# Output products by blocks in three more chunks of a fused Performer and MLP kernel, with w_out's sums streamed in and added on GpSimd

## The chip, the cores and the metric

The kernel runs on one core of a Trainium2 chip. The metric is the device time of one execution in microseconds (us), taken as the median of several runs. The engines are named as in the profile: PE is TensorE (PEld its weight loads), DVE is VectorE, ACT is ScalarE, POOL is GpSimd, SP is SyncE, whose queue issues nearly all DMAs here.

## The reference

Attention with positive random features (batch 8, 8 heads, sequence 576, head dimension 64, 128 features), whose result, laid out as 4608 rows of 512, goes through an MLP:

```python
def phi(x):
    proj = np.einsum('bhsd,md->bhsm', x, omega)
    h = proj - np.sum(x * x, axis=-1, keepdims=True) / 2.0
    h = h - np.max(h, axis=-1, keepdims=True)
    return np.exp(h) / np.sqrt(m)
q_p, k_p = phi(q * scale), phi(k * scale)
kv  = np.einsum('bhsm,bhsd->bhmd', k_p, v)
z   = np.sum(k_p, axis=2)
num = np.einsum('bhsm,bhmd->bhsd', q_p, kv)
den = np.einsum('bhsm,bhm->bhs', q_p, z)[..., None] + 1e-06
x   = (num / den).transpose(0, 2, 1, 3).reshape(4608, 512)
h   = x @ w_in                                  # 512 x 2048
out = (h * np.tanh(np.log1p(np.exp(h)))) @ w_out   # 2048 x 512
```

## The kernel before

**Number format.** Every large matrix is held as two fp16 parts, a high part and a rest, and a product takes three matmuls: high by rest, rest by high, high by high. The high parts are casts, mostly on ACT; the rests are a subtraction (`rest`, lines 83 and 85), on DVE for the MLP's activations `g` and `gb`, on GpSimd for `sk`, `sq`, `xs` and `vb`.

**Chunks.** The 4608 rows are 18 chunks of 256. The main loop (line 1284) runs over c = 2 to 17; "iteration c" below means one pass of it. It interleaves two generators: the input product of chunk c (`ff_in`, 8 steps of 24 matmuls 128x256, PE row `ph` of line 770) and the output product of chunk c-1 (`ff_out`, 8 steps of 12 matmuls 128x512, PE row `po` of line 1097). A string of the letters i and o sets the order, one letter for one step. After a number of letters the loop makes a `step()`, which lets the tasks on an agenda emit what is due: the attention of later chunks (k tasks: `pk`, `ek`, `kp`, `pkv`; q tasks: `pq`, `eq`, `qn`, `qp`, `pn`, then `x`), casts and rests. A scheduler then orders what was emitted for each engine; each engine and each queue runs its own list strictly in order.

**Products by blocks.** From chunk 15 (`SC0`, `SO0`) both products are made by the Strassen-Winograd scheme: the operands are cut into 2 by 2 blocks, and seven products of half the size in each direction replace eight. The left and right operands are then blocks (`a11`, `b11` ...) or sums of blocks (`s1` to `s4` of the left, `t1` to `t4` of the right). `ff_in7` makes the input product so, `ff_out7` the output product: 7 products `q_*` of 24 matmuls 128x256 (line 1044), two o steps each. Its left blocks are the tiles `gb`, made by `g_blocks` (casts, 4 subtractions or additions of line 985 for each pair of h tiles, and 14 rests); its results are put together by additions into two `o` tiles (line 1053), each stored once it is whole. The sums of w_in and of w_out are made earlier, in the loop's iterations 4 to 14 (`sums_make`, 10 additions of 128x512 for each of eight pieces, line 806, on DVE) and written to DRAM. `ask_sum` fetches the sums of w_in through a ring of three places (line 878); `fetch_t` fetches all of w_out's sums into tiles that the attention no longer needs (`tw`, line 1015).

**x of the chunks by blocks.** A chunk that takes its input product by blocks needs x transposed in four pieces: the first tile of 128 rows, the second, and two of differences. `x_sums` (line 638) makes the differences `tt` in place and in a tile of the tag "o", and `x_send` sends each piece: a cast into an `xs` tile (2 buffers), the rest on GpSimd, and a transposing DMA from SP (line 616):

```python
tt = sb.tile([P, 2, H * D // 2], F32, tag="o", name=f"tt{c}", bufs=2)
```

The tag "o" has two buffers in SBUF. In `ff_out` an `o` tile lives from its cast at the end of the chunk to its store. In `ff_out7` both are taken at the chunk's start and live to its end. PSUM has three groups: `ps_h` (2 banks: `ph`), `ps_o` (2: `po`, `q_*`), and `ps_a` (4), which serves all of the attention (`pk`, `pq`, `pkv`, `pt`, `pn`) and the products `p_*` of `ff_in7`.

Of the kernel before, what the change touches and what calls it, by code (L numbers as in the profile page):

```python
# [30 lines left out]
def tile_kernel(  # L31
# [11 lines left out]
    P = 128  # L43
# [707 lines left out]
    def ff_in(c):  # L751

        must(2, "x", c)
        sp = [(b_scales(b) if c else None, lo, hi) for b, lo, hi in spans(c * CH, CH)]
        for gr in range(FT // FG):
            gT[c, gr] = sb.tile([P, 2, FG, CH], F16, tag="g", name=f"g{c}_{gr}", bufs=GB)
            for q in range(FG // FQ):
                if c:
                    h = sb.tile([P, FQ, CH], F32, tag="ht", name=f"h{c}_{gr}_{q}", bufs=HB)
                else:  # L760
                    h = g0(gr)[:, q * FQ:(q + 1) * FQ]
                for j in range(0, FQ, 2):
# [12 lines left out]
                    if c == 0:  # L775

                        later(1, cast, act, h[:, j:j + 2, :], ph)
                        if gr == FT // FG - 1 and q == FG // FQ - 1 and j > 0:
                            later(2, mish0)
                    else:  # L780
                        later(1, mish, sp, h[:, j:j + 2, :], ph)
                        if j > 0:
                            later(2, g_split, c, gr, q, sp, h)
                    yield


# [10 lines left out]
    def sums_make(key, blocks, first, shape):  # L797
# [5 lines left out]
        b11, b12, b21, b22 = blocks  # L803

        def tt(out, in0, in1, op=ALU.subtract):
            dve.tensor_tensor(out=out, in0=in0, in1=in1, op=op)
# [196 lines left out]
    def fetch_t():  # L1003
# [7 lines left out]
        for i, (tag, n) in enumerate(places):  # L1011
            t = sb.tile([P, n, 2, BW // 2], F16, tag=tag, name=f"tw{i}", bufs=bufs[tag])
            for u in range(n):
                op, j = units.pop(0)
                nc.sync.dma_start(out=t[:, u], in_=sums["w", j, op])  # L1015
                tsum[op, j] = t[:, u].rearrange("p a (f m) -> p a f m", f=2)

    def ff_out7(c):
        sp = [(b, lo // 2, hi // 2) for b, lo, hi in spans(c * CH, CH)]
        us = o_scale(sp[0][0])[:, 2:3]  # L1020
        if len(sp) > 1:
            mixed = const.tile([P, 1], F32, name=f"uso{c}")
# [8 lines left out]

        def products(name, right):
            n, i = GAT[name]
            own, tag = ((ps_h, "h"), (ps_o, "o"))[nth[0] % 2]
            nth[0] += 1
            ps = own.tile([P, DM // 2], F32, tag=tag, name=f"q_{name}_{c}")
            for f in range(FG):
                must(1, "gb", c, name, f // FQ)
                for a, y in ((1, 0), (0, 1), (0, 0)):
                    if right in full:  # L1040
                        rhs = wo_block(f // 2, y, *full[right])[:, f % 2]
                    else:
                        rhs = tsum[right, f // 2][:, y, f % 2]
                    nc.tensor.matmul(  # L1044
                        out=ps, lhsT=gT[c, n][:, i, a, f, :], rhs=rhs,
                        start=f == 0 and (a, y) == (1, 0), stop=f == FG - 1 and (a, y) == (0, 0),
                    )
# [236 lines left out]
    for c in range(2, NCH):  # L1284
        fi = (ff_in if c < SC0 else ff_in7)(c)
        fo = (ff_out if c <= SO0 else ff_out7)(c - 1)
        order = "io" * 8 if c < SC0 else ("iioiioioioi" if c == SC0 else ORD[c - SO0 - 1]) * 2
        if c == SO0:
            at(slot[0] + 8, fetch_t)
        for j, what in enumerate(order):  # L1290
            if j % 2 == 0 and given[0] < min(pace(c + j / len(order)), len(items)):
                give()
# [53 lines left out]
```

## Time and profile before

| | |
|---|---|
| median of 3 runs | 941.36 us (940.48 to 941.49) |
| the profiled execution | 939.57 us, span 937.8 us |
| PE busy | 920.5 us, 98% of the span |
| PEld busy | 689.4 us, 74% |
| DVE busy | 707.1 us, 75% |
| ACT busy | 658.9 us, 70% |
| POOL busy | 213.6 us, 23% |
| TensorE clock granted, mean | 0.993 |
| DMA | 108.69 MB, mean 116 GB/s |

The difference of 1.8 us between the profiled execution and its span lies before the first and behind the last instruction. In the timeline of PE, iteration 12 begins at 653.0 us, 13 at 701.9, 14 at 751.4, 15 at 799.8 and 16 at 842.

A row of the profile reads: line, engine, operation, out<-in by the program's names, shape, count, then busy time, the mean of one, and the idle time ahead of it with what ended it. In a timeline the first number is the start, the second the duration of the group. DMA issues end with the median time from issue to landing.

### The profile page before, as it was taken

How to read it: one execution, taken by the hardware profiler on the slowest of the kernel's cores; microseconds unless marked ns; L12 is line 12 of the kernel's file. 1: busy time of each engine (PE TensorE's matmuls, PEld its weight loads, DVE VectorE, ACT ScalarE, POOL GpSimd, SP SyncE). 2: the span in 40 equal slices, each digit the busy share in tenths (PEclk: the TensorE clock that was granted, in tenths of full speed). 3: DMA queues.
4: the chain of work that ended last, by engine and by line, in shares of the span. 5: the costliest groups of instructions: out<-in, count | busy, mean ns of one | idle time of the engine just before them, and what ended most of it. 6: DMA issues, size and time to landing. Idle time of an engine off the chain costs nothing. (4 is left out here: it accounts for less than half of the span.)

```text
span 937.8 us, 21111 instructions
## 1 busy us (share of the span) xinstructions
PE 920.5 (98%) x8795; PEld 689.4 (74%) x8795; DVE 707.1 (75%) x1234; ACT 658.9 (70%) x873; POOL 213.6 (23%) x134
## 2 busy tenths in 40 slices
PE   9799989999999999999999999999999999999998
PEld 6688765677777777777777777777777777679997
DVE  5799898685678688787688857878688756658774
ACT  6568966678777878778677776788786866345442
POOL 0000023242342224321333134231241232200000
PEclk9799999999999999999999999999999999999999
DMA  9766325443442256323543265523533156973521
GB/s 308 264 227 215 108 58 93 99 83 75 95 107 85 80 115 128 90 81 76 107 114 97 69 120 107 126 60 93 112 73 91 35 114 141 210 218 92 162 66 45
DMA packets 153055, 108.69 MB, mean 116 GB/s; under 512 B 112832, under 2 KB 125248, under 8 KB 152960
## 3 DMA queue, kind: packets, MB, share of 16 engines
q1 hardware_dynamic: 152640, 106.75, 44.6%
q8 instruction: 69, 1.13, 0.5%
q10 hardware_dynamic: 320, 0.59, 0.2%
q14 instruction: 26, 0.21, 0.1%
HBM read 63.14 MB, written 17.83 MB: 86 GB/s over the span
## 5 line engine op out<-in xcount | busy, mean ns | idle before, releaser
L770 PE MATMUL ph<-xT,w 128*128 128x256 f16 (+1 forms) x2816 | 342.2, 278 | 0.0
L1097 PE MATMUL po<-wo,g 128*128 128x512 f16 x1344 | 308.5, 379 | 0.0
L770 PEld LDWEIGHTS <-w 128*128 128x128 f16 x2688 | 260.7, 98 | 46.1 <-issue 0.6
L1097 PEld LDWEIGHTS <-g 128*128 128x128 f16 x1344 | 127.2, 98 | 132.7
L83 POOL TENSOR_TENSOR sq<-fq,sq 64x1024 f16<-64x1024 f32 x31 | 70.5, 2275 | 253.6 <-ACT sq L74 177.8
L955 ACT ACTIVATE h<-ph,us 128x512 f32<-128x512 f32 (+3 forms) x152 | 83.2, 573 | 49.7 <-PE ph L770 48.5
L85 DVE SCALAR_TENSOR_TENSOR g<-h,us,g 128x1024 f16<-128x1024 f32 (+3 forms) x76 | 99.9, 1325 | 15.2 <-ACT g L74 14.9
L83 POOL TENSOR_TENSOR sk<-fk,sk 64x1152 f16<-64x1152 f32 x24 | 59.3, 2469 | 91.6 <-ACT sk L74 79.3
L83 POOL TENSOR_TENSOR xs<-x,xs 128x512 f16<-128x512 f32 (+1 forms) x35 | 40.7, 1164 | 153.0 <-DVE xs L76 102.0
L955 ACT ACT_TABLE_LOAD x56 | 71.8, 1283 | 1.0
L441 ACT ACT_TABLE_LOAD x53 | 68.0, 1283 | 4.2 <-DVE ek L435 3.3
L426 DVE TENSOR_REDUCE mxq<-pq 128x4 f32<-128x512 f32 x72 | 46.7, 682 | 24.8 <-PE pq L401 23.9
L83 DVE TENSOR_TENSOR qn<-eq,qn 128x1024 f16<-128x1024 f32 x31 | 39.2, 1263 | 29.9 <-ACT qn L74 29.9
L906 PEld LDWEIGHTS <-w 128*128 128x128 f16 x1008 | 59.0, 98 | 3.3 <-issue 0.7
L441 ACT ACTIVATE ek<-ek,lnt 128x1152 f32<-128x1152 f32 x24 | 30.1, 1256 | 42.3 <-DVE ek L435 42.2
L74 ACT ACTIVATE g<-h,us 128x1024 f16<-128x1024 f32 (+3 forms) x64 | 58.2, 932 | 0.8
L426 DVE TENSOR_REDUCE mxk<-pk 128x4 f32<-128x512 f32 (+1 forms) x96 | 49.5, 546 | 7.3 <-PE pk L416 3.5
L83 DVE TENSOR_TENSOR kp<-ek,kp 128x1152 f16<-128x1152 f32 x24 | 32.8, 1366 | 27.0 <-ACT kp L74 26.2
L1044 PEld LDWEIGHTS <-gb 128*128 128x128 f16 x504 | 48.3, 98 | 5.2
L83 POOL TENSOR_TENSOR vb<-vf,vb 128x640 f16<-128x640 f32 x24 | 37.3, 1554 | 55.2 <-DVE vb L76 41.5
L955 ACT ACTIVATE h<-h,us 128x1024 f32<-128x1024 f32 (+2 forms) x16 | 14.7, 930 | 48.6 <-DVE h L915 48.6
L441 ACT ACTIVATE eq<-eq,lnt 128x1024 f32<-128x1024 f32 x31 | 35.6, 1149 | 18.8 <-DVE eq L435 18.5
(185 smaller groups left out, 1370.3 us busy)
## 6 DMA issues: line engine op xcount, KB each, us to landing
w<-ds SPq DMA_DIRECT2D x48, 256.0 KB, 3.6
vf<-in_vL_dram SPq DMA_DIRECT2D x32, 325.0 KB, 3.3
out_dram<-o SPq DMA_DIRECT2D x36, 256.0 KB, 2.3
fq<-in_qT_dram SPq DMA_DIRECT2D x31, 256.0 KB, 3.5
fk<-in_kT_dram SPq DMA_DIRECT2D x24, 256.0 KB, 3.6
raw<-in_w_out_dram SPq DMA_DIRECT2D x5, 1024.0 KB, 7.8
wo<-in_w_in_dram SPq DMA_DIRECT2D x4, 1024.0 KB, 10.6
raw<-in_w_in_dram SPq DMA_DIRECT2D x4, 1024.0 KB, 15.3
```

The costliest lines, as they stand in the source:

```text
L74: act.activation(out, in_, AF.Copy, scale=scale)
L83: eng.tensor_tensor(out=out, in0=in_, in1=hi, op=ALU.subtract)
L85: eng.scalar_tensor_tensor(out=out, in0=in_, scalar=scale, in1=hi, op0=ALU.mult, op1=ALU.subtract)
L426: sub = dve.tensor_reduce(out=mx[:, lo:hi], in_=pp[:, :m, :], axis=AX.X, op=ALU.max, negate=by_act)
L441: last = act.activation(e, e, AF.Exp, bias=lnt)
L770: nc.tensor.matmul(out=ph[:, i, :], lhsT=wi(a, k, f) if c else wi0(k, f), rhs=xT[c][:, y, k, :] if c else xT0()[:, k, :], start=n == 0, st ...
L906: nc.tensor.matmul(out=ph[:, i, :], lhsT=left(gr, op_l, i, a, k), rhs=x_region(c, r)[:, y, k0 + k, :], start=n == 0, stop=n == len(mm) - 1,)
L955: act.activation(h[:, :, lo:hi], ph[:, :, lo:hi], AF.Mish, scale=us[:, 0:1])
L1044: nc.tensor.matmul(out=ps, lhsT=gT[c, n][:, i, a, f, :], rhs=rhs, start=f == 0 and (a, y) == (1, 0), stop=f == FG - 1 and (a, y) == (0, 0),)
L1097: nc.tensor.matmul(out=po[i], lhsT=gT[c, gr][:, a, f % FG, i * P:(i + 1) * P], rhs=wo(y, f), start=f == 0 and (a, y) == parts[0], stop=f = ...
```

## The change

- `SO0` goes from 15 to 12: chunks 12, 13 and 14 take their output product by blocks too. Their input product stays as it was, so `ff_in` now starts `g_blocks` for them in place of `g_split`. In iterations 13 and 14 (output of chunks 12 and 13) the order has 8 i and 14 o; iteration 15 (output of 14) has 14 i and 14 o, where it had 14 i and 8 o.
- The sums of w_out for these chunks are not all held: each is streamed (`ask_t`, two DMAs of 128 KB for each of the four j) into the place of the block `b12` of w_out, which no product reads, as soon as the previous sum has been used there.
- The seven products of chunks 12 and 13 use the two `ps_o` banks only (chunk 14's and later ones alternate between `ps_h` and `ps_o`).
- The additions of `sums_make`, for w_in and w_out alike, go from DVE to GpSimd (line 811 after).
- `fetch_t` is called in iteration 15 as before; its loads land for chunk 15's output product. A scale tile is reused (`spare`).

```diff
-    SO0 = 15
+    SO0 = 12
@@ ff_in
+        hs = {}
         for gr in range(FT // FG):
-            gT[c, gr] = sb.tile([P, 2, FG, CH], F16, tag="g", name=f"g{c}_{gr}", bufs=GB)
+            if c < SO0:
+                gT[c, gr] = sb.tile([P, 2, FG, CH], F16, tag="g", name=f"g{c}_{gr}", bufs=GB)
...
-                        if j > 0:
+                        if j > 0 and c < SO0:
                             later(2, g_split, c, gr, q, sp, h)
+                        elif j > 0:
+                            start(g_blocks(c, gr, q, hs), 2)
@@ sums_make
         def tt(out, in0, in1, op=ALU.subtract):
-            dve.tensor_tensor(out=out, in0=in0, in1=in1, op=op)
+            pool.tensor_tensor(out=out, in0=in0, in1=in1, op=op)
@@
+    T_OPS = ("t3", "t2", "t1", "t4")
+    t_uses = [(c, op) for c in range(SO0, SC0) for op in T_OPS]
+    def ask_t(j):
+        n = t_asked.get(j, 0)
+        t_asked[j] = n + 1
+        if n < len(t_uses):
+            for a in range(2):
+                nc.sync.dma_start(
+                    out=wo_block(j, a, 0, 1),
+                    in_=sums["w", j, t_uses[n][1]][:, a].rearrange("p (f m) -> p f m", f=2),
+                )
@@ ff_out7, products
-            own, tag = ((ps_h, "h"), (ps_o, "o"))[nth[0] % 2]
+            own, tag = ((ps_h, "h"), (ps_o, "o"))[nth[0] % 2 if c + 1 >= SC0 else 1]
...
+                    elif c < SC0:
+                        rhs = wo_block(f // 2, y, 0, 1)[:, f % 2]
...
+                if f % 2 == 1 and right not in full and c < SC0:
+                    ask_t(f // 2)
@@ main loop
-        order = "io" * 8 if c < SC0 else ("iioiioioioi" if c == SC0 else ORD[c - SO0 - 1]) * 2
+        order = "io" * 8 if c <= SO0 else "ioioiooioiooioiooioioo" if c < SC0 else (
+            "iioiioioioi" if c == SO0 == SC0 else ORD[max(0, c - SC0 - 1)]
+        ) * 2
+        if c == SC0:
+            at(slot[0] + 8, fetch_t)
         if c == SO0:
-            at(slot[0] + 8, fetch_t)
+            must(FT // 4, "tsums")
+            for j in range(4):
+                at(slot[0] + 9 + j, ask_t, j)
```

**Where the rows stand now.** Three places show how the lists moved. The first is DVE's list in iteration 14, around the differences `tt15` of chunk 15's x (names carry the chunk or tile and a running number). Before:

```order
L588 TENSOR_TENSOR x31_9748<-pn31_0_9750,rd31_9749 128x256
L588 TENSOR_TENSOR x31_9748<-pn31_1_9775,rd31_9749 128x256
L638 TENSOR_TENSOR tt15_9827<-x31_9748,x30_8879 128x256
L638 TENSOR_TENSOR tt15_9827<-x31_9748,tt15_9827 128x256
L638 TENSOR_TENSOR x31_9748<-x31_9748 128x256
L638 TENSOR_TENSOR x30_8879<-x30_8879,tt15_9827 128x256
L76 CAST xs15_1_9832<-x31_9748 128x512
L76 CAST xs15_2_9863<-tt15_9827 128x512
```

Now:

```order
L1080 SCALAR_TENSOR_TENSOR o13_0_9845<-q_s4_13_10461,warm_74,o13_0_9845 128x256
L990 TENSOR_TENSOR h14_0_1_9924<-h14_1_1_10295,h14_0_1_9924 128x512
L85 SCALAR_TENSOR_TENSOR gb14_2_10370<-h14_0_0_9815,us6_8966,gb14_2_10370 128x512
L85 SCALAR_TENSOR_TENSOR gb14_2_10370<-h14_1_0_10109,us6_8966,gb14_2_10370 128x512
L990 TENSOR_TENSOR h14_0_1_9924<-h14_0_1_9924 128x512
L83 TENSOR_TENSOR qn34_10458<-eq34_10340,qn34_10458 128x1024
L638 TENSOR_TENSOR tt15_10048<-x31_9968,x30_8903 128x256
L85 SCALAR_TENSOR_TENSOR gb14_3_10376<-h14_1_0_10109,us6_8966,gb14_3_10376 128x512
L638 TENSOR_TENSOR tt15_10048<-x31_9968,tt15_10048 128x256
L638 TENSOR_TENSOR x31_9968<-x31_9968 128x256
L638 TENSOR_TENSOR x30_8903<-x30_8903,tt15_10048 128x256
L76 CAST xs15_1_10053<-x31_9968 128x512
```

`tt15` stood right behind the two rows that make x31. It now stands behind the last addition into the first output tile of chunk 13 (`o13_0`), and its first row waits for the store of that tile, whose buffer of the tag "o" it takes; the end of `gb14`, of chunk 14's activations, is now around it.

The second is SP's queue from there on, at the change from iteration 14 to 15. Before (`tw` are loads of `fetch_t`, `xT` and `xm` the pieces of x, `qp` the transposed features of a q tile, the rows of line 878 the ring):

```order
L616 DMA_TRANSPOSE xT15_8409<-xs15_1_9832 128x8x128
L616 DMA_TRANSPOSE xm15_2_9900<-xs15_2_9863 128x8x128
L878 DMA w3_105<-ds2_0_1_7504 128x2x512
L616 DMA_TRANSPOSE xm15_3_9939<-xs15_3_9902 128x4x128
L1015 DMA tw5_10667<-dt1_w_2_5096 128x1024
L1015 DMA tw5_10667<-dt1_w_3_5846 128x1024
L616 DMA_TRANSPOSE xT16_9482<-xs16_0_9995 128x8x128
L558 DMA_TRANSPOSE qp33_10026<-qn33_9970 128x16x128
L1129 DMA out_dram<-o13_0_10127 128x512
```

Now:

```order
L1097 DMA out_dram<-o13_0_9845 128x512
L1035 DMA wo_101<-dt3_w_0_3842 128x2x256 x2
L1035 DMA wo_101<-dt3_w_1_4685 128x2x256 x2
L1035 DMA wo_101<-dt3_w_2_5472 128x2x256 x2
L558 DMA_TRANSPOSE qp34_10508<-qn34_10458 128x16x128
L1035 DMA wo_101<-dt3_w_3_6231 128x2x256 x2
L616 DMA_TRANSPOSE xT15_8408<-xs15_1_10053 128x8x128
L616 DMA_TRANSPOSE xm15_2_10135<-xs15_2_10104 128x8x128
L1035 DMA wo_101<-dt2_w_0_3592 128x2x256
L616 DMA_TRANSPOSE xm15_3_10178<-xs15_3_10137 128x4x128
```

The transposes of x15 stood ahead of the store of `o13_0`; they now stand behind it, behind `qp34`, and among the streamed sums of line 1035. Then follow, in this order, both pieces `xT16` and `xm16_2`, the store of `o13_1`, `xm16_3`, four ring loads, `xT17_0`, `qp35`, and after it `t1`, eight loads of `tw` and `t4`.

The third is DVE's list in iteration 13, from the scores of the k product `pk7_1` to the rest `kp7_1` that its product `pkv7_1` on PE waits for. Before:

```order
L435 TENSOR_TENSOR ek7_1_9062<-pk7_1_4_9073,mxk7_1_9063 128x128
L426 TENSOR_REDUCE mxk7_1_9063<-pk7_1_5_9076 128x4
L85 SCALAR_TENSOR_TENSOR g13_0_8947<-h13_0_0_8948,us5_7600,g13_0_8947 128x4x128
L435 TENSOR_TENSOR ek7_1_9062<-pk7_1_5_9076,mxk7_1_9063 128x512
L85 SCALAR_TENSOR_TENSOR g13_0_8947<-h13_0_0_8948,us6_8942,g13_0_8947 128x4x128
L83 TENSOR_TENSOR kp7_1_9140<-ek7_1_9062,kp7_1_9140 128x1152
```

Now:

```order
L435 TENSOR_TENSOR ek7_1_9139<-pk7_1_4_9150,mxk7_1_9140 128x128
L426 TENSOR_REDUCE mxk7_1_9140<-pk7_1_5_9153 128x4
L435 TENSOR_TENSOR ek7_1_9139<-pk7_1_5_9153,mxk7_1_9140 128x512
L1080 SCALAR_TENSOR_TENSOR o12_0_8997<-q_a12_12_9170,us5_7600,o12_1_8998 128x256
L85 SCALAR_TENSOR_TENSOR gb13_0_9194<-h13_0_0_8971,us5_7600,gb13_0_9194 128x4x64
L85 SCALAR_TENSOR_TENSOR gb13_0_9194<-h13_0_0_8971,us6_8966,gb13_0_9194 128x4x64
L83 TENSOR_TENSOR kp7_1_9215<-ek7_1_9139,kp7_1_9215 128x1152
```

The two rests of `g13` are now rests of `gb13` of half the size, behind the last row of `ek7_1` rather than around it, and an addition of chunk 12's output stands ahead of them. Between `pk7_1` and `pkv7_1`, PE had 3 groups of 12 `po`, 2 of 24 `ph` and the 18 of `pk7_2`; it now has 48 matmuls `q_*` of 128x256, 2 groups of 24 `ph` and the 18 of `pk7_2`.

More of the change, by code (lines that the diff above doesn't have):

```diff
@@ L759, in ff_in @@
                     h = sb.tile([P, FQ, CH], F32, tag="ht", name=f"h{c}_{gr}_{q}", bufs=HB)
+                    hs[gr, q] = h
                 else:
@@ L1016, in fetch_t @@
                 tsum[op, j] = t[:, u].rearrange("p a (f m) -> p a f m", f=2)
+    spare = [warm]
+    T_OPS = ("t3", "t2", "t1", "t4")
+    t_uses = [(c, op) for c in range(SO0, SC0) for op in T_OPS]
+    t_asked = {}
+    def ask_t(j):
[7 more added lines that the diff above has]
+                )
     def ff_out7(c):
@@ L1021, in ff_out7 @@
         if len(sp) > 1:
-            mixed = const.tile([P, 1], F32, name=f"uso{c}")
+            mixed = spare.pop() if spare else const.tile([P, 1], F32, name=f"uso{c}")
             for b, lo, hi in sp:
@@ L1041, in products @@
                         rhs = wo_block(f // 2, y, *full[right])[:, f % 2]
+                    elif c < SC0:
+                        assert t_uses.index((c, right)) == t_asked[f // 2] - 1
+                        rhs = wo_block(f // 2, y, 0, 1)[:, f % 2]
                     else:
```

## The prediction

> **What bounds the kernel now.** I read the page's busy time and digits first, then PE's waits, then a table by iteration.
>
> ```profile
> PE 920.5 (98%) x8795; PEld 689.4 (74%) x8795; DVE 707.1 (75%) x1234; ACT 658.9 (70%) x873; POOL 213.6 (23%) x134
> PE   9799989999999999999999999999999999999998
> ```
>
> PE is busy 98% of the span and full from the eighth slice on. PE's waits between 640 and 842 us, where iterations 12 to 15 lie, are two:
>
> ```profile
> PE p_s L906 <- DVE h L915: 0.6, 1, 0.6
> PE pn L572 <- DMA qp<-qn: 0.5, 1, 0.5
> ```
>
> So PE sets the time, a matmul taken away is worth its time, and no other edit here can gain more than these 1.1 us. A new wait costs its full length. The table by stretch (PE, PEld, DVE, ACT, POOL, clock, DMA share, GB/s) shows iterations 13, 14 and 15:
>
> ```profile
> 702.00:751.00 49.00, 49.00 (x468) 35.36 (x466) 37.29 (x51) 36.51 (x52) 11.67 (x7) 1.00 0.21 60
> 751.00:800.00 49.00, 48.48 (x469) 34.50 (x466) 29.89 (x55) 32.49 (x34) 13.60 (x9) 1.00 0.60 130
> 800.00:842.00 42.00, 41.43 (x489) 29.97 (x487) 25.03 (x54) 16.31 (x28) 5.11 (x5) 1.00 0.91 224
> ```
>
> No other engine is full, but in iteration 15 the DMA engines are 0.91 busy.
>
> **The matmuls: -7.1 us.** Starts in PE's timeline give what each group takes (start, duration, group):
>
> ```profile
> 796.32 1.06 PE L401 MATMUL pq<-om,sq 128*128 128x128 f16 x16
> 797.21 2.75 PE L1097 MATMUL po<-wo,g 128*128 128x512 f16 x12
> 799.80 2.84 PE L906 MATMUL p_a<-xT,w 128*128 128x128 f16 x48
> 802.48 0.91 PE L572 MATMUL pn<-kv,qp 128*128 128x65 f16 x24
> 803.23 2.75 PE L1097 MATMUL po<-wo,g 128*128 128x512 f16 x12
> ...
> 842.84 1.47 PE L1044 MATMUL q_a<-wo,gb 128*128 128x256 f16 x12
> 844.15 1.50 PE L906 MATMUL p_a<-xT,w 128*128 128x128 f16 x24
> ```
>
> Twelve `po` take 799.80 - 797.21 = 2.59 us, twelve `q_` 844.15 - 842.84 = 1.31. A chunk's output goes from 8 x 2.59 = 20.7 to 14 x 1.31 = 18.3, and three chunks from 62.2 to 55.0: -7.1 with the rounding. The other groups move but keep their size: `pq` 0.89, 24 `p_` 1.34 (half of 2.68), `pn` 0.75.
>
> **The new work on DVE and ACT.** Chunk 12, 13 and 14 each get 14 rests (28 of half the width where a chunk spans two batches, as 13 does), 8 additions of h blocks and 8 of output, in place of 4 or 8 rests of `g`:
>
> ```profile
> L85 DVE SCALAR_TENSOR_TENSOR gb<-h,us,gb 128x512 f16<-128x512 f32 x28 | 20.4, 745 | 0.9 <-ACT gb L74 0.2
> L985 DVE TENSOR_TENSOR h<-h 128x512 f32<-128x512 f32 x12 | 8.3, 689 | 4.1 <-ACT h L955 3.9
> L1053 DVE SCALAR_TENSOR_TENSOR o<-q_s,us,o 128x256 f32<-128x256 f32 x12 | 5.6, 480 | 5.8 <-PE q_s L1044 5.7
> L85 DVE SCALAR_TENSOR_TENSOR g<-h,us,g 128x1024 f16<-128x1024 f32 x36 | 58.6, 1627 | 9.9 <-ACT g L74 9.9
> L83 DVE TENSOR_TENSOR qn<-eq,qn 128x1024 f16<-128x1024 f32 x31 | 39.2, 1263 | 29.9 <-ACT qn L74 29.9
> ```
>
> That is 14 x 0.745 + 8 x 0.69 + 8 x 0.48 - 4 x 1.63 = +13 us a chunk, in iterations where DVE has 12 to 19 us free: no bound by its sum, but its queue gets longer where PE waits for it. The tight place is the k product `pkv7_1` in iteration 13:
>
> ```profile
> 710.68 1.17 PE L401 MATMUL pk<-om,sk 128*128 128x128 f16 x18
> 711.68 2.75 PE L1097 MATMUL po<-wo,g 128*128 128x512 f16 x12
> 725.75 1.13 PE L522 MATMUL pkv<-vb,kp 128*128 128x65 f16 x30
> ...
> 724.34 1.36 DVE L83 TENSOR_TENSOR kp<-ek,kp 128x1152 f16<-128x1152 f32 x1 [3.50 <-ACT kp L74]
> ```
>
> PE had 14.0 us of other work from `pk` (done 711.68) to `pkv` (725.75), and DVE's `kp` ended at 725.70: no slack. Now PE has 48 x 0.109 + 2 x 2.62 + 1.0 = 11.5 us there. If the way over DVE and ACT stays 14.0 long, PE waits 2.5 us. The way held one block of 2.1 us that need not return (next part), which leaves none to 0.4. `pkv7_3` stands likewise. Bounds 0 and 5; I take **+1.3**, nearer to the way without the block.
>
> **The sums' additions on GpSimd.** One row of the 80 that leave DVE, what a like operation takes on POOL, and the three rows in which DVE and POOL meet:
>
> ```profile
> L806 DVE TENSOR_TENSOR s<-s,w 128x512 f32<-128x512 f32 x12 | 8.3, 688 | 0.3
> L83 POOL TENSOR_TENSOR xs<-x,xs 128x512 f16<-128x512 f32 x32 | 38.4, 1200 | 140.2 <-DVE xs L76 89.2 <-issue 38.8 <-ACT xs L74 11.6
> ...
> 716.66 2.36 POOL L83 TENSOR_TENSOR sk<-fk,sk 64x1152 f16<-64x1152 f32 x1 [2.58 <-ACT sk L74]
> 716.75 2.83 DVE L85 SCALAR_TENSOR_TENSOR g<-h,us,g 128x512 f16<-128x512 f32 x1
> 720.10 0.74 DVE L85 SCALAR_TENSOR_TENSOR g<-h,us,g 128x512 f16<-128x512 f32 x1
> ```
>
> DVE loses 80 x 0.69 = 55 us or more, POOL gets 80 x 1.2 = 96, spread over ten iterations. DVE's time was not on PE's path, so this gains at most the 1.1 us above. But a `g` rest that starts just behind POOL's `sk` takes 2.83 us, where the next takes 0.74: POOL holds DVE up for the length of its operation. Each of 80 new additions can hold DVE up by 1.2 us, and `sk`, from which `pk` comes, now queues behind up to three of them. Covered by DVE's free time except at the k products without slack; bounds -1 and +10 (half a microsecond at each of 20 k tasks), I take **+0.5**. The Trainium skill's page "SBUF — State Buffer", section "Who interferes with whom", calls this an exclusive lock and says "Whoever issues first gets the shared pair for the whole instruction": by that a POOL addition would also wait for a running rest of DVE. The trace agrees for the first direction (2.83 against 0.74); the second would make the additions later and leave my sum as it is, since the sums of w_out are due in iteration 12 only.
>
> **Streaming w_out's sums.** PE's list leaves 4.6 us or more from the last use of a place to the first use of the next sum in chunks 12 and 13. `tw` loads of twice the size landed in 3.4 us between 751 and 800, so nothing waits; were it 5.6, as later, each of 8 sums could cost 1. I take 0. In iteration 15 these loads stand in SP's queue among the transposes, which comes next.
>
> **The way of x15 to x17: +8.5 us.** The differences `tt15` take a buffer of the tag "o". Chunk 13's two output tiles now hold both from the start of iteration 14 to its end, so `tt15`, which ran at 768.02, must wait for the store of `o13_0`, and everything behind it on DVE too. PE waits for what hangs on it: the four `ps_a` banks hold `pn32` and `pn33` until DVE makes x32 and x33, and x33 must wait for x16's first piece, since `xs` has two buffers, each freed by a transpose's landing. The rows:
>
> ```profile
> 768.02 0.41 DVE L638 TENSOR_TENSOR tt<-x,x 128x256 f32<-128x256 f32 x1
> 769.48 0.42 DVE L76 CAST xs<-x 128x512 f16<-128x512 f32 x1
> ...
> 772.35 1.25 SPq L616 DMA_TRANSPOSE xT<-xs  x1
> 805.54 1.67 SPq L558 DMA_TRANSPOSE qp<-qn  x1
> 812.43 0.91 PE L572 MATMUL pn<-kv,qp 128*128 128x65 f16 x24
> ...
> out_dram<-o SPq DMA_DIRECT2D x36, 256.0 KB, 2.3
> xT<-xs SPq DMA_TRANSPOSE x34, 3.1
> qp<-qn SPq DMA_TRANSPOSE x31, 4.3
> xm<-xs SPq DMA_TRANSPOSE x6, 3.3
> ```
>
> From T, the end of `q_s4_13` on PE, at the means above: the addition 0.5; DVE's five rows ahead of `tt15` 0.69 + 0.75 + 0.75 + 0.69 + 1.26, so 4.6 (the store, landed at 2.8, is covered); four rows of L638 1.46, a rest 0.75 and a cast 0.34 make 7.15; POOL's `xs15_1` 8.35, `xs15_2` 9.55; the transpose `xT15` lands at 11.45, `xm15_2` at 12.9. Then the cast `xs16_0` 13.25 and x33 13.65, when `p_a11_15` may start. PE's work to there is 91 `q_` and `pq35`, 10.8: **2.9 late**. On: `tt16` and `xs16_1` 16.45, `xT16_0` landed 17.55, `xs16_2` on POOL 19.1, `xm16_2` landed 22.4, `xs17_0` on POOL 23.95, `xT17_0` issued until 25.2, `qp35` behind it in SP's queue, landed 29.5. PE reaches `pn35` after 138 `q_` (15.0), `pq` 0.89, five `p_` 6.7 and `pn34` 0.75 = 23.4: **6.1 late** in all. Before, `tt15` to `pn35` (812.43) had 44.4 us. The upper end: landings as between 800 and 842,
>
> ```profile
> xm<-xs SPq DMA_TRANSPOSE x3, 4.8
> xT<-xs SPq DMA_TRANSPOSE x2, 6.4
> qp<-qn SPq DMA_TRANSPOSE x1, 5.3
> ```
>
> add 1.8 at x15, 3.3 at `xT16_0`, 1.5 at `xm16_2` and 1.0 at `qp35`: 13.7 late. Those came beside ten `tw` loads, of which eight now stand behind `qp35`, so I stay near the lower end, 7.5. These eight then stand ahead of `t4` in the queue, which chunk 14's last product needs: one more. 8.5 in all, bounds 4 and 16 (the first if DVE's rows overlap better than I add them).
>
> **Sum.** -7.1 + 1.3 + 0.5 + 8.5 = +3.2: the profiled execution goes from 939.57 to 942.8, and the median, which stands 1.8 above it, from 941.36 to **944.6**. What a measurement can tell from no change is about 0.2%, 1.9 us.
>
> **The rivals.** *The way of x is hidden.* If `tt15` gets its buffer earlier, or if PE's list holds enough behind T, only the first two prices stay: 941.36 - 7.1 + 1.8 = 936.1. For it speaks that the kernel before lost only 1.1 us in all these iterations with queues as intertwined; against it that six landings of 2.3 to 4.3 in a row are 20 us by themselves, and PE has 23.4. Chance 0.28, 934 to 939.4. *It is half hidden*, 3.5 to 6 us late: 939.5 to 943.2, no difference to be told, chance 0.15. *The DMA engines are full:* the landings of the last fence hold and `t4` and the ring come late too; 941.36 - 7.1 + 1.8 + 16 = 952, for it the 0.91 with some 5 MB more to fetch in that stretch; chance 0.08. *GpSimd is the bound of iterations 4 to 13:* additions ahead of `sk` and blocked DVE rows cost 10 us; 941.36 - 7.1 + 1.3 + 8.5 + 10 = 954; it decides once a k task is late by over 0.5 us each time. Against it POOL's 23%; chance 0.05.
>
> **How the numbers follow.** The forecast, 943.2 to 949.5, has 0.44; it, the full DMAs and GpSimd make slower 0.57, hidden makes faster 0.28, half hidden 0.15. Cases of both signs hold much, so the range runs from 935.5 to 951; the forecast's own is 943.2 to 949.5.
>
> **What would show it.** Right: PE's groups of the output are 1.31 for twelve, and PE has a gap of about 3 us ahead of `p_a11_15` and more ahead of `pn35`, released by DVE's x33 and by `qp<-qn`; `tt` rows start behind a store of `o`. Small gaps ahead of `pkv` in iteration 13. Wrong: a PE as full as before in iteration 15 (hidden), or gaps ahead of `pk` in iterations 4 to 12 (GpSimd).

## The result and the profile after

The changed kernel takes 978.8 us (median of 4 runs, 978.35 to 982.89), the kernel before 940.9 beside it: a ratio of 1.041 (95% interval 1.039 to 1.043), so 38 us slower. The forecast was 944.6, in a range up to 951. The side was right; of the size the forecast had less than a tenth (3.2 of 38 us). The matmuls' 7.1 us alone would have given 940.9 - 7.1 = 933.8; against that, 45.0 us were lost elsewhere.

The page of the changed kernel: busy times, PE's digits, and the clock that PE was granted.

```profile
PE 930.4 (95%) x9011; PEld 719.9 (73%) x9011; DVE 720.3 (73%) x1244; ACT 674.4 (69%) x910; POOL 332.2 (34%) x214
PE   9799999999999999999999999999988898797998
PEclk9799999999999999999999999999999999798999
```

Two things are to be seen in the first row. PE's idle time went from 937.8 - 920.5 = 17.3 us to 981.1 - 930.4 = 50.7, so 33.4 more. And PE was busy for longer, though it had less to do: 920.5 - 7.1 = 913.4 were to be expected, and 17.0 more were taken. The third row fits that: in late slices the granted clock is not full. The two add up to 50.4 and not to 45.0, since the profiled execution of the changed kernel (982.9 us) lies above its median, and that of the kernel before (939.6) below.

The same in stretches (PE, PEld, DVE, ACT, POOL, clock, DMA share, GB/s), from iteration 12 on:

```profile
653.00:702.00 49.00, 49.00 (x460) 35.28 (x459) 35.68 (x70) 43.00 (x53) 21.86 (x13) 1.00 0.54 124
702.00:756.00 54.00, 47.79 (x499) 39.81 (x497) 47.42 (x68) 39.47 (x58) 29.24 (x18) 1.00 0.39 102
756.00:812.00 56.00, 52.83 (x624) 47.10 (x623) 47.42 (x89) 45.22 (x63) 8.49 (x4) 1.00 0.67 175
812.00:850.00 38.00, 29.48 (x321) 26.47 (x319) 27.89 (x57) 15.38 (x20) 9.98 (x8) 0.90 0.86 192
850.00:872.00 22.00, 17.58 (x233) 16.21 (x234) 11.82 (x26) 6.63 (x13) 0.00 (x0) 0.81 0.95 276
872.00:900.00 28.00, 22.92 (x278) 21.33 (x277) 21.66 (x42) 11.66 (x24) 4.56 (x3) 0.87 0.71 181
```

Between 702 and 756 us DVE is busy 47.4 of 54 us, where it was 37.3 of 49. From 812 on the clock is 0.81 to 0.90. What PE waits for, over the whole span (us in total, times, longest; rows of the kernel's start are left out):

```profile
PE pn L572 <- DMA qp<-qn: 8.5, 4, 4.5
PE pkv L522 <- DVE kp L83: 8.0, 4, 2.5
...
PE p_s L911 <- DVE h L920: 5.1, 1, 5.1
PE p_a L911 <- DVE x L588: 2.8, 1, 2.8
PE q_s L1069 <- ACT o L74: 2.2, 1, 2.2
PE q_a L1069 <- DMA wo<-dt_w: 1.9, 1, 1.9
PE p_a L911 <- DVE eq L435: 1.8, 1, 1.8
PE pk L401 <- DVE ek L435: 1.7, 1, 1.7
PE q_a L1069 <- DVE gb L85: 1.5, 1, 1.5
```

No single wait explains the loss: these are nine rows of 1.5 us and more, and two of the attention (`pn`, `pkv`) lead. Of the first row, 2.2 us at 142 and 160 us stand in the kernel before as well. The gaps of iteration 15 that the prediction named are there in PE's timeline: 2.8 us ahead of `p_a11_15`, released by x33, and 4.5 ahead of `pn35`:

```profile
829.74 2.74 PE L911 MATMUL p_a<-xT,w 128*128 128x128 f16 x24 [2.78 <-DVE x L588]
835.84 2.65 PE L911 MATMUL p_a<-xT,w 128*128 128x128 f16 x24 [1.81 <-DVE eq L435]
852.09 1.50 PE L572 MATMUL pn<-kv,qp 128*128 128x65 f16 x24 [4.51 <-DMA qp<-qn]
853.40 2.75 PE L911 MATMUL p_s<-xT,w 128*128 128x128 f16 x24
```

Behind each gap the groups are slow as well: 24 `p_a` or `p_s` take 2.65 to 2.75 us, where they took 1.50 before (by the same column).

### The profile page after: what moved, and what is told of

It is laid out like the page before. It is cut to its first block, busy times and chain, and to the rows that moved or that the text cites. A ratio compares the mean times of both kernels' runs of the same rounds, so it can differ in the third digit from the quotient of the medians.

```text
span 981.1 us, 21823 instructions
## 1 busy us (share of the span) xinstructions
PE 930.4 (95%) x9011; PEld 719.9 (73%) x9011; DVE 720.3 (73%) x1244; ACT 674.4 (69%) x910; POOL 332.2 (34%) x214
## 4 chain that ended last, share of the span: by engine, by line
PE 70%; DVE 13%; DMA 7%; ACT 4%; POOL 3%; issue 2%; SPq 1%; POOLq 0%; ACTq 0%; DVEq 0%
PE ph L773 25%; PE po L1124 19%; PE q_s L1069 5%; PE p_s L911 3%; PE q_a L1069 3%; PE pq L401 3%; DVE gb L85 2%; PE pn L572 2%; PE p_a L911 2%; POOL sw L811 2%; DMA qp<-qn 2%; PE pkv L522 2%; PE pk L401 2%; PE pkv L490 1%; PE po L1141 1%
## 5 line engine op out<-in xcount | busy, mean ns | idle before, releaser
L773 PEld LDWEIGHTS <-w 128*128 128x128 f16 x2688 | 261.6, 98 | 46.5 <-issue 2.4
L1124 PE MATMUL po<-wo,g 128*128 128x512 f16 x1056 | 242.5, 379 | 0.0
L1124 PEld LDWEIGHTS <-g 128*128 128x128 f16 x1056 | 100.0, 98 | 104.2
L1069 PEld LDWEIGHTS <-gb 128*128 128x128 f16 x1008 | 97.3, 99 | 19.4 <-issue 6.3
L83 POOL TENSOR_TENSOR xs<-x,xs 128x512 f16<-128x512 f32 (+1 forms) x35 | 44.2, 1263 | 169.0 <-DVE xs L76 126.1
L85 DVE SCALAR_TENSOR_TENSOR g<-h,us,g 128x1024 f16<-128x1024 f32 (+3 forms) x60 | 77.4, 1301 | 17.9 <-ACT g L74 17.7
L74 ACT ACTIVATE gb<-h,us 128x512 f16<-128x512 f32 (+3 forms) x112 | 66.8, 645 | 32.3 <-DVE h L990 22.3
L85 DVE SCALAR_TENSOR_TENSOR gb<-h,us,gb 128x512 f16<-128x512 f32 (+3 forms) x112 | 78.1, 730 | 2.4 <-ACT gb L74 1.5
L911 PEld LDWEIGHTS <-w 128*128 128x128 f16 x1008 | 64.9, 104 | 11.8 <-issue 5.8
L83 DVE TENSOR_TENSOR kp<-ek,kp 128x1152 f16<-128x1152 f32 x24 | 38.1, 1586 | 21.7 <-ACT kp L74 21.7
L960 ACT ACTIVATE h<-h,us 128x1024 f32<-128x1024 f32 (+2 forms) x16 | 14.7, 930 | 50.7 <-DVE h L920 50.7
L1069 PE MATMUL q_s<-wo,gb 128*128 128x256 f16 x360 | 44.7, 273 | 2.9 <-ACT o L74 2.2
```

What stands on the lines that cost most here:

```text
L74: act.activation(out, in_, AF.Copy, scale=scale)
L83: eng.tensor_tensor(out=out, in0=in_, in1=hi, op=ALU.subtract)
L85: eng.scalar_tensor_tensor(out=out, in0=in_, scalar=scale, in1=hi, op0=ALU.mult, op1=ALU.subtract)
L773: nc.tensor.matmul(out=ph[:, i, :], lhsT=wi(a, k, f) if c else wi0(k, f), rhs=xT[c][:, y, k, :] if c else xT0()[:, k, :], start=n == 0, st ...
L911: nc.tensor.matmul(out=ph[:, i, :], lhsT=left(gr, op_l, i, a, k), rhs=x_region(c, r)[:, y, k0 + k, :], start=n == 0, stop=n == len(mm) - 1,)
L960: act.activation(h[:, :, lo:hi], ph[:, :, lo:hi], AF.Mish, scale=us[:, 0:1])
```

## The experiments

### One suspect at a time: the o buffers and GpSimd

The first four runs shared a chip, with the kernel before at 940.3. The **o buffers**: `tt` takes a buffer whose tiles are no longer read, so nothing waits for the stores of `o13_0` and `o14_0`.

```diff
-        tt = sb.tile([P, 2, H * D // 2], F32, tag="o", name=f"tt{c}", bufs=2)
+        tt = sb.tile([P, 2, H * D // 2], F32, tag="kv", name=f"tt{c}", bufs=3)
```

> The changed kernel (978.8 us), but the differences tt of x15 to x17 take a buffer of the attention's tag kv, whose tiles of earlier batches are no longer read, and not of the tag o; so tt15 and tt17 need not wait for the stores of o13_0 and o14_0. Theory 1 (the o buffers): the gaps of PE from the end of iteration 14 into iteration 16 (1.5 + 2.8 + 1.8 + 4.5 + 1.9 + 0.2 + 5.1 = 17.8 us, of DVE x, DVE eq, DMA qp and DVE h) go, and with them the lower granted clock there (0.90, 0.81, 0.87 between 812 and 900 us): 948 to 953. Rival (SP's queue and the DMA engines, 0.86 to 0.95 busy there, are what is late): the gaps stay, 968 or more.

Measured: 975.5 us (ratio 1.038, 1.035 to 1.042), 3.3 faster, which is less than the spread of its runs (972.9 to 978.2). `tt15` ran at 781.7 in place of 818.6, and the waits for x33, for `eq` and for `h` went. But the time did not go with them: PE then waited 8.0 us for `qp` and 9.0 for the streamed sums in the same iterations. The theory falls as an account of the loss: the chain was real, yet freeing it only showed the next ones, which were late nearly as much.

**GpSimd**: the additions of the sums back on DVE in the changed kernel, and, the other way round, moved to GpSimd alone in the kernel before.

```diff
         def tt(out, in0, in1, op=ALU.subtract):
-            pool.tensor_tensor(out=out, in0=in0, in1=in1, op=op)
+            dve.tensor_tensor(out=out, in0=in0, in1=in1, op=op)
```

> The changed kernel, but the additions of the sums of w_in and w_out stay on DVE. Theory 2 (GpSimd): the gaps ahead of pk and pkv at 306, 310, 436 and of pn at 612 us (1.7 + 0.7 + 2.3 + 1.7 = 6.4 us) go: 970 to 973, with iteration 12 reached about 8 us earlier. Rival (these gaps come from elsewhere, the other order of the rows): within 2 us of 978.8.

> The kernel before, with nothing changed but that the additions of the sums go to GpSimd. Theory 2: 6 to 9 us slower, 947 to 950, with gaps ahead of pk, pkv or pn between 300 and 620 us. Rival (the additions are free there; the order of the changed kernel makes the gaps): 939 to 942.

Measured: 969.4 with them back on DVE (9.4 faster; ratio 1.031, 1.028 to 1.034), and 947.7 for the kernel before with them on GpSimd alone (7.4 slower; ratio 1.008, 1.007 to 1.010). The first lies 0.6 below the range of the theory, the second in it. The 9.4 us are what is left of two effects: with the additions in DVE's list again, PE's wait ahead of `pkv7_1` in iteration 13 grew from 2.5 to 5.2 us. With no other change than the additions on GpSimd, PE waits like this (2.2 us of the first row were there before):

```profile
PE pn L572 <- DMA qp<-qn: 4.7, 4, 1.9
PE pkv L522 <- DVE kp L83: 3.9, 3, 1.8
...
PE pk L401 <- DVE ek L435: 1.4, 1, 1.4
```

How an addition on GpSimd makes a k product late is seen in the changed kernel at 304 us. DVE's list has the rest `t_w` of a sum ahead of the last `ek`:

```profile
301.19 0.68 DVE L426 TENSOR_REDUCE mxk<-pk 128x4 f32<-128x512 f32 x1
303.83 2.05 DVE L83 TENSOR_TENSOR t_w<-sw,t_w 128x512 f16<-128x512 f32 x1 [1.97 <-ACT t_w L74]
305.81 0.68 DVE L435 TENSOR_TENSOR ek<-pk,mxk 128x512 f32<-128x512 f32 x1
```

The rest waits 1.97 us for ACT's cast, which waits for POOL's addition (until 303.1), and then takes 2.05 us where such a rest takes 0.68 at its shortest, beside POOL's `sq` (303.2 to 305.3). `ek` is some 3.4 us late (1.97 and 1.4), and PE's second half of `pk` waits 1.72. So the additions cost in two ways: they hold DVE up while both run, and the longer way of a sum holds up what stands behind its rest in DVE's list. This, and not POOL's share of 34%, is the price.

Both edits together:

> Both of these edits on the changed kernel. If theories 1 and 2 hold and add up: 940 to 946, what is left over the wished 934 being the gaps of iteration 13 (pkv 2.5 + 2.5, q_s 2.2, ph 1.0). If the two losses overlap, more.

Measured: 966.1 (ratio 1.027, 1.026 to 1.029). The two losses add up (9.4 and 3.3 of 12.7 us), and are less than a third of the 45.0; the expected 940 to 946 is missed by 20. This kernel is the base of what follows. Its waits from 640 us on:

```profile
PE pn L572 <- DMA qp<-qn: 8.0, 2, 4.1
PE pkv L522 <- DVE kp L83: 5.7, 2, 5.2
PE q_a L1069 <- DMA wo<-dt_w: 4.5, 1, 4.5
PE q_s L1069 <- DMA wo<-dt_w: 4.3, 3, 2.1
PE ph L773 <- ACT h L960: 0.6, 1, 0.6
```

### The streamed sums

Four runs with the kernel before at 940.2. First the stream is left out: nothing is fetched, and the products read what lies there.

```diff
         if n < len(t_uses):
-            for a in range(2):
-                nc.sync.dma_start(out=wo_block(j, a, 0, 1), ...)
+            pass
```

> Base of this run and the next three: the changed kernel with tt in the tag kv and the sums' additions on DVE (966.1 us). Here the streamed sums of w_out are not fetched at all in chunks 12 to 14 (the products read the block b12 that lies there, so these chunks' outputs are not the reference's); all other work is done. Theory 3 (SP's queue and the landings of the stream set what is left): the waits for wo<-dt_w (8.8 us) go, those for qp<-qn (8.0 us) mostly too since 96 issues of 0.5 us leave SP's queue, and the lower clock with them: 942 to 948. Rival (DVE and ACT are what is late, by the new rests and additions): only the waits for wo<-dt_w and some clock go, 952 to 957, with the waits for qp<-qn and pkv<-kp as before.

Measured: 952.7 (ratio 1.013, 1.012 to 1.015), so the stream costs 13.4 us, and what it leaves is at the edge of the rival's range. The waits for `wo` are gone, and those of the attention are not:

```profile
PE pn L572 <- DMA qp<-qn: 8.1, 2, 4.6
PE pkv L522 <- DVE kp L83: 6.1, 2, 5.2
PE ph L773 <- ACT h L960: 0.7, 1, 0.7
```

So there are two losses: the stream, and an attention that is late without it too. SP's queue has a share in the second at one place. Ahead of `pn34` the transpose of `qp` is issued as soon as DVE's rest ends (808.9 and 809.0 us); ahead of `pn35` it is issued 1.7 us later than that (823.4 and 825.1), behind a ring load, and its issue takes 3.12 us in place of 1.78. Why the stream is late, the base's queue shows at the end of iteration 15 (SP's rows, and then PE's):

```profile
847.75 4.95 SPq L1020 DMA_DIRECT2D tw<-dt_w  x10
854.41 1.20 SPq L616 DMA_TRANSPOSE xm<-xs  x1
855.65 2.12 SPq L1035 DMA_DIRECT2D wo<-dt_w  x4
...
860.11 4.43 PE L1069 MATMUL q_a<-wo,gb 128*128 128x256 f16 x20 [4.46 <-DMA wo<-dt_w]
```

Ten loads of `tw` take 4.95 us to issue and stand ahead of `t4`; PE waits 4.46 us for it. Two runs tested this place, one with half as many issues and then one with `fetch_t` five steps later:

```diff
-            for a in range(2):
-                nc.sync.dma_start(out=wo_block(j, a, 0, 1), in_=...)
+            nc.sync.dma_start(
+                out=slots[NB + 1 + j].rearrange("p a (f m) -> p (a f) m", f=2)[:, :, DM // 2:],
+                in_=sums["w", j, t_uses[n][1]].rearrange("p a (f m) -> p (a f) m", f=2),
+            )
@@ late_tw, besides
-            at(slot[0] + 8, fetch_t)
+            at(slot[0] + 13, fetch_t)
```

> The base with one DMA of 256 KB for each streamed sum in place of two of 128 KB: the same bytes, half of the issues (48 in place of 96). If SP's issue time (0.5 us each, 24 us less) is what makes the stream and qp late: 3 to 8 us faster than 966.1, 958 to 963. If the bytes or the landings are: within 2 us.

> one_dma (964.3 us) with fetch_t five steps later in iteration 15, so that the loads of tw stand behind the streamed sums t4 of chunk 14 in SP's queue and not ahead of them. If their place in the queue made t4 late: the wait q_a<-wo (2.9 us at 859) goes and the clock behind it, 959 to 962. If DMA bandwidth did: within 1.5 us of 964.3, or a new wait for tw in iteration 16.

Measured: 964.3 (ratio 1.027, 1.025 to 1.029), then 959.6 (1.021, 1.019 to 1.024; the kernel before at 939.7 in that batch). Half the issues are worth 1.8 us, less than expected and hardly clear of the noise: within what "the bytes or the landings" allowed. The median landing went from 3.2 us for 128 KB to 4.2 for 256 KB. The later place of `tw` in the queue is worth 4.7 more, as expected, and the wait `q_a<-wo` is gone. Some 7 of the 13.4 us are left, with waits of 0.2 to 1.9 us for single sums.

### Fewer chunks

> The base with SO0 = 14: only chunk 14 takes its output product by blocks in addition. The matmuls then save 2.4 us and not 7.1. If each further chunk by blocks costs more than it saves in waits (theory: DVE, ACT and SP have no room for it beside the attention): 941 to 948, so less than a third of the loss of 25.8, since iterations 13 and 14 are as before. If one chunk is enough to bring the whole loss (the meeting of streams with the fetch of tw in iteration 15): 955 or more.

> The base with SO0 = 13: chunks 13 and 14 by blocks. Between so14 and 966.1; if the loss goes with the number of chunks, about 956. If iteration 13 with its k products (pkv waits 5.2 us and the clock behind them) is what chunk 12 adds: 966.1 less some 8, 958.

Measured: 950.9 for one chunk (ratio 1.012, 1.010 to 1.013) and 960.7 for two (1.022, 1.020 to 1.025), against 966.1 for three. One chunk already costs 10.7 us, a little over the expected 941 to 948, with a wait of 3.9 for `wo` and one of 3.2 for the ring's `w`, both in iteration 15, with the clock behind them. The second costs 9.8, and two together are 3 to 5 us above what was expected; the third costs 5.4. None of the three pays.

### Why the attention is late

The tight place of the prediction, `pkv7_1`, in no_stream: DVE's and PE's rows. The way is the time from the end of `pk` on PE over DVE and ACT to `pkv`; PE's cover is the other work that it has in between.

```profile
720.63 0.69 DVE L811 TENSOR_TENSOR s<-w,w 128x512 f32<-128x512 f16 x1
721.24 0.88 DVE L426 TENSOR_REDUCE mxk<-pk 128x4 f32<-128x512 f32 x2
...
731.11 1.36 DVE L83 TENSOR_TENSOR kp<-ek,kp 128x1152 f16<-128x1152 f32 x1 [4.61 <-ACT kp L74]
```

```profile
714.65 1.17 PE L401 MATMUL pk<-om,sk 128*128 128x128 f16 x18
715.65 2.78 PE L1065 MATMUL q_a<-wo,gb 128*128 128x256 f16 x24
...
732.52 1.83 PE L522 MATMUL pkv<-vb,kp 128*128 128x65 f16 x30 [5.22 <-DVE kp L83]
```

`pk` is done at 715.65, but DVE takes it up at 721.24 only, 5.6 us later (2.9 in the kernel before): eight rows stand ahead, six of them of the last sums, which in turn stand behind rests of `gb` and additions of h. The way takes 16.9 us, where it was 14.1 before; PE's cover is 11.7, where it was 14.1. So the wait of 5.2 us is 2.8 of longer way and 2.4 of shorter cover.

In the changed kernel itself, with the sums on GpSimd, PE waits 2.5 us ahead of `pkv7_1` and as long ahead of `pkv7_3`:

```profile
744.50 1.13 PE L522 MATMUL pkv<-vb,kp 128*128 128x65 f16 x30 [2.51 <-DVE kp L83]
...
765.97 1.13 PE L522 MATMUL pkv<-vb,kp 128*128 128x65 f16 x30 [2.48 <-DVE kp L83]
```

The way to `pkv7_1` is 16.5 us there too (`pk` is done at 728.00), but 2.2 of it lie under another wait of PE, for ACT's `o`. Three runs took one cause away each.

The rests left out (no DVE work for them, the same PE work), on no_stream:

```diff
-            for us, lo, hi in sp:
+            for us, lo, hi in sp if c >= SC0 else []:
                 rest(dve, g[:, 1, fs, lo:hi], src[:, :, lo:hi], g[:, 0, fs, lo:hi], us[:, 1:2])
@@ products
-                        out=ps, lhsT=gT[c, n][:, i, a, f, :], rhs=rhs,
+                        out=ps, lhsT=gT[c, n][:, i, a if c >= SC0 else 0, f, :], rhs=rhs,
```

> no_stream (952.7 us), and of the activations' blocks of chunks 12 to 14 only the high parts are made: their rests (some 10 to 13 us of DVE a chunk) are left out, and the products read the high part in their place, so PE's work is the same. The waits left in no_stream are pkv<-kp 6.1 and pn<-qp 8.1 us. Theory 5 (DVE's longer queue makes the attention late): both fall to under 4 together, 937 to 944. Rival (the shorter cover by PE alone, ACT and SP unchanged): they stay above 8 together, 948 to 952.

Measured: 942.6 (ratio 1.002, 1.001 to 1.003), 10.1 us faster than no_stream, in the range of the DVE theory. But the two waits did not fall to 4 together; they are 8.3, as the rival had it:

```profile
PE pn L572 <- DMA qp<-qn: 7.2, 4, 2.6
PE pkv L522 <- DVE kp L83: 1.1, 1, 1.1
```

The k product has its slack back; the q tiles are still late, in four waits of up to 2.6 us in place of two of up to 4.6. So DVE's rests are worth 10.1 us, of which 6.4 are idle time of PE and most of the others the clock; 8.8 us stay over 933.8 with neither stream nor rests, with the additions of h and of the output still there and PE's cover still shorter. These two were not taken apart.

More cover for the attention, by moving its tasks:

```diff
-        return 15 + (c - 1) * 4.0 if c < 5 else 31.0 + (c - 5) * 3.8
+        return 15 + (c - 1) * 4.0 if c < 5 else 31.0 + (c - 5) * 4.0
@@ k_task, ahead of pkv
-        yield gap("kv", f"k{b}_{hp}")
+        yield gap("kv", f"k{b}_{hp}") + (1 if b == 7 else 0)
@@ q_task, ahead of pn
-        yield 2
+        yield 3 if t >= 30 else 2
```

> Base again tt in kv, sums on DVE (966.1 us). Only the places of the attention's tasks are moved: its items are handed out a little earlier (4.0 in place of 3.8 a chunk), the product pkv of the last batch one step later after its kp, and pn one step later after qp from tile 30 on. PE's list then has 20.3 us of work between pk7_1 and pkv7_1 (11.5 in the base, 14.0 in the kernel before) and 20.0 between pq34 and pn34 (14.4; 17.3 before). Theory 4 (the way from pk or pq over DVE and ACT takes 17 to 19 us there, 13.5 to 14 before, and PE's shorter products cover less of it): the waits pkv<-kp (5.7 us) and pn<-qp (8.0) fall to under 3 together, and 4 us of clock go: 948 to 954. Rival (DVE or SP is full there, so the way gets longer as well): the waits stay within 3 us of what they were, 962 or more.

> no_stream (952.7 us) with the wide gaps, which took 8.5 us off the base. If the stream and the attention's lateness are separate: 942 to 946, and what is left over 934 is the wait for qp that moved to tile 33 (5.9 us) and its clock. If wide gaps only helped because they moved SP's queue: 950 or more.

Measured: 957.6 (ratio 1.019, 1.017 to 1.021), 8.5 faster than the base, and 947.2 (1.008, 1.006 to 1.010), 5.5 faster than no_stream; both gained less than was expected, by 3.6 and 1.2 us. The waits for `pkv` are gone in both, as expected; those for `qp` are not: in the first, 5.9 us now lie ahead of `pn33` and 2.0 ahead of `pn35`, and a wait of 4.5 us for the ring's `w` is new. Cover is a cause, then, but what is moved away from one place is partly late at the next.

The last sums out of iteration 13, by making all sums faster:

```diff
-        at(slot[0] + 40 + 19 * i, lambda fn=fn, arg=arg: start(fn(*arg)))
+        at(slot[0] + 40 + 14 * i, lambda fn=fn, arg=arg: start(fn(*arg)))
```

> The base with the sums of w_in and w_out made at every 14th step in place of every 19th, so that DVE's last row of them lies ahead of pk7_0 and not in iteration 13. If DVE's backlog by these rows is what made pkv7_1 5.2 us late: that gap goes to under 2, 958 to 962, with the waits for qp<-qn as they were. If the new rests and additions alone are enough: within 2 us of 966.1.

Measured: 974.9 (ratio 1.037, 1.034 to 1.039), 8.8 **slower** than the base, the other way than forecast. The gap of 5.2 us ahead of `pkv7_1` did go (the largest wait for `kp` is 1.3): with the sums out of DVE's list there, the way took 7.3 us (730.46 to 737.72), well under the cover. So taking this backlog away is enough there. But with the sums denser, DVE is late at 372, 389 and 614 us (waits of 1.1 to 3.8 for `qp` or `ek`), where the base had none.

### The clock

On no_stream, 30 useless matmuls of 128x260 fill most of the waits ahead of `pn34` and `pn35`:

```diff
+            if t >= 34 and g == 0:
+                for _ in range(30):
+                    nc.tensor.matmul(
+                        out=pn, lhsT=idle[:, 0:P], rhs=idle[:, 0:4 * D1].rearrange("p (i d) -> p i d", i=4),
+                        start=True, stop=True,
+                    )
```

> no_stream (952.7 us) with 30 useless matmuls 128x260 (3.3 us of PE at full clock) written into the bank of pn34 and of pn35 ahead of their own matmuls, where PE waits 4.6 and 3.5 us for qp. Theory 6 (idle time itself lowers the clock behind it, as the rows after each long gap show): PE's waits shrink by what the useless matmuls take, and the groups behind run at full speed (24 p_s in 1.3 in place of 2.5, 24 q_a in 2.6 in place of 3.4 us): 948.5 to 951.5. Rival (the slow groups have another cause, or the matmuls push the rest): 952.5 to 956.

Measured: 954.6 (ratio 1.016, 1.014 to 1.018), 2.0 slower than no_stream: the rival's range. Where it worked as meant, at `pn35`, the clock did stay up. First no_stream, then the filled kernel:

```profile
829.85 1.50 PE L572 MATMUL pn<-kv,qp 128*128 128x65 f16 x24 [3.51 <-DMA qp<-qn]
831.16 2.50 PE L911 MATMUL p_s<-xT,w 128*128 128x128 f16 x24
```

```profile
813.33 0.92 PE L578 MATMUL pn<-kv,qp 128*128 128x65 f16 x24 [1.87 <-DMA qp<-qn]
816.06 2.65 PE L917 MATMUL p_a<-xT,w 128*128 128x128 f16 x24 [1.81 <-DVE eq L435]
...
830.38 0.91 PE L578 MATMUL pn<-kv,qp 128*128 128x65 f16 x24
832.44 1.50 PE L917 MATMUL p_s<-xT,w 128*128 128x128 f16 x24
```

With the wait filled, 24 `p_s` take 1.50 in place of 2.50 us, and the granted clock over them is 1.00 in place of 0.56. At `pn34` the useless matmuls left 1.87 us of the wait and another of 1.81 came, since the list of PE was ordered anew, and the clock fell as before. So that idle time brings the clock down is shown at one place; that filling it gains time is not.

### Putting it together

> All edits together, three chunks by blocks: tt in kv, sums on DVE and early, one DMA for each streamed sum, tw late, wide gaps. If the losses found so far are all there is and add up: 966.1 less 12 to 16 (gaps), 2 (one DMA), 3 to 5 (tw): 943 to 949, a little slower than the kernel before; under 940 would mean that the matmuls' 7 us come through.

> The base with wide gaps, one DMA for each streamed sum and tw late: 966.1 - 8.5 - 1.8 - 4.7 = 951 if the three add up, the best of the complete kernels with three chunks; 955 or more if late tw takes away what wide gaps had gained.

> so14 (950.9 us) with one DMA for each streamed sum and tw late. Its waits are wo<-dt_w 3.9 and w<-ds 3.2 us in iteration 15, with the lower clock behind each. If both come from SP's queue filled with tw: 941 to 945; to beat the kernel before (939.7) all of it must go. If w<-ds stays: 946 to 948.

Measured: 966.0 for all edits on three chunks (ratio 1.028, 1.026 to 1.031, 17 us above what was expected; it has the early sums, which cost), 957.6 without early sums (1.020, 1.017 to 1.022), and 945.9 for one chunk with a single DMA and late `tw` (1.006, 1.004 to 1.008). The gains do not add up: wide gaps and late `tw` together are worth what wide gaps were alone. The best complete kernel with a further chunk is still 0.6% slower than the kernel before, with a wait of 3.4 us for a streamed sum and one of 1.4:

```profile
PE q_s L1068 <- DMA wo<-dt_w: 4.9, 2, 3.4
```

No version beats the kernel before.

## Why the prediction was right on the side and wrong on the size

The 45.0 us between 978.8 and 933.8, by the medians: GpSimd 9.4, the o buffers 3.3, the stream 13.4, DVE's rests 10.1, the rest 8.8. The first two were taken away in the complete kernel, the next two from what was left, so their sizes hold in this order. The steps that failed are three prices: the new work on DVE, the additions on GpSimd and the stream stood in the sum at 1.3, 0.5 and 0, and taking them away gained 10.1, 9.4 and 13.4 us.

- **"What bounds the kernel now": right, with a gap.** PE did set the time and every new wait was paid. "A new wait costs its full length" was too little: it costs more. In the row from the changed kernel over the base and no_stream to no_stream_no_rests, PE idled 33.4, 22.4, 13.5 and 7.1 us more than before, and its matmuls took 17.0, 11.1, 7.3 and 3.9 us longer than 913.4: about half a microsecond of slower matmuls for each of idle time. The ratio is not a constant: it is a quarter in late_tw (5.1 for 20.4) and nearly one in so14 (6.6 for 6.9, with 918.1 to be expected for one chunk). The prediction had no term for it. The kernel before with the additions on GpSimd, where the new gaps are at most 1.9 us, shows no such time (PE busy 920.9, against 920.5).
- **"The matmuls: -7.1 us": right.** Twelve `q_` in place of twelve `po` take 1.31 where nothing disturbs them (745.47 to 746.78).
- **"The new work on DVE and ACT", +1.3: failed.** The work itself was sized well: 13 us a chunk forecast, 40.1 us more of DVE in the base, so 13.4 a chunk. Its mechanism was named, "its queue gets longer where PE waits for it", with `pkv7_1` as the place, 2.5 us as the price of a way that stays as long as it was, and 5 as the upper bound. In the changed kernel 2.51 and 2.48 us came at `pkv7_1` and `pkv7_3`: the bound, and not the 1.3. The step went wrong in three ways. The way was taken to be at most as long as before, since the block by POOL need not return; it got 2.4 to 2.8 longer, for what queued ahead of `mxk`. The free time of 12 to 19 us was read as room, though it is an average, and PE waits for a row's place in the list. And only the k products were priced here: in the base and in no_stream the q tiles 34 and 35 lost 8 us in waits. Measured, 10.1 for the rests alone, and 18.9 with the part that was not taken apart.
- **"The sums' additions on GpSimd", +0.5: too small.** 7.4 alone, 9.4 here. The bound of 10 and the rival ("additions ahead of `sk` and blocked DVE rows cost 10 us") had the right size, and got a chance of 0.05, because POOL's 23% was read against it. The prediction's own sign for it, a gap ahead of `pk` in iterations 4 to 12, came with 1.72 us at 306.55. The way was partly another: not `sk` behind additions, but `ek` behind a sum's rest that waits for POOL.
- **"Streaming w_out's sums", 0: wrong.** 13.4. The time from ask to use was compared with a landing, and the queue between them was left out: the loads are issued by SP in order, at half a microsecond each, behind `tw` and behind waits. The prediction did see `tw` ahead of `t4`, and took 1 for it; 4.7 were measured by moving `tw`.
- **"The way of x15 to x17", +8.5: the gaps came, the price did not.** Ahead of `p_a11_15` 2.8 us were measured for the forecast 2.9. That is luck in part: from T (814.31) the way took 15.4 us and not 13.65, and PE came 12.7 after T and not 10.8, held up by a wait of 1.5 for `gb`; the two errors cancel. At `pn35` all waits of the way (1.5, 2.8, 1.8 and 4.5) make 10.6. But taking the cause away gained 3.3 only, since `qp` and the stream were late in the same iterations. A wait is worth its length only if nothing behind it is late as well.
- **The rivals.** "Hidden" and "half hidden" fell. The full DMA engines and GpSimd were each priced alone, at 952 and 954; what came was several at once, which the prediction had kept apart.

On the clock, the Trainium skill's page "TensorE: Matmul & The Clock Gate", section "What's actually happening", has PE's clock fall to half after an idle window of about 3.4 us, on windows that run freely. The direction agrees: 24 `p_s` took 2.75 us at 853.40, against 1.50, and the granted clock from 852 to 856 us was 0.50. The length does not: gaps of 2.78 and, six microseconds later, 1.81 us were enough at 829.74 and 835.84. Gaps of 2.2 to 2.5 us between 735 and 766 left the groups behind them at full speed, and so did one of 3.11 us in sums_dve ahead of the same `p_a`:

```profile
817.59 1.51 PE L911 MATMUL p_a<-xT,w 128*128 128x128 f16 x24 [3.11 <-DVE x L588]
```

Whether windows decide that, no run here tells.

## What to carry to other kernels

Where one engine is 98% busy, price an edit by what shrinks under the neighbours' waits: fewer matmuls are less cover for every chain that runs beside them, and each chain (here k, q, x and the stream) needs its own sum of way against cover, in the list order of the engine that serves it, not by that engine's average load. Work out the lateness of all chains that meet in one stretch: taking away the first one found gains little while the next is late nearly as much. Leave room for a slower clock behind gaps of several microseconds; here it added between a quarter and nearly the whole of the idle time, and mostly about half. An operation moved to an idle engine must also be asked what stands behind its consumer on the engine that it left.

## What the hardware showed that was not expected

- The length of a gap alone does not tell whether the clock of TensorE falls behind it: after 2.8 us, 24 matmuls of 128x128 took 2.74 in place of 1.50 us, while gaps of 2.2 to 2.5 us elsewhere, and one of 3.1 in sums_dve, had no such effect.
- A DMA of 128 KB costs SP's queue half a microsecond to issue (4 in 2.12 us), as one of 256 KB does (10 in 4.95 us): the issue time goes with the count and hardly with the bytes. Yet half as many issues for the same bytes gained only 1.8 us of 966.
- A rest on DVE took 2.05 us beside POOL's `sq`, and additions on POOL took up to 2.27 us where their shortest is 1.15: the first is DVE held up beside POOL, the second fits POOL held up beside DVE, but was not followed row by row.
